# Linear attention and a token/channel mixer: token mixing two slots sooner, phi of q behind it, loads in one burst per batch

## The chip, the core and the metric

The kernel runs on one core of one Trainium2 chip. The metric is device time of one execution in microseconds (us). The kernel before takes 286.91 us, the median of three runs (286.29 to 287.79).

A core has TensorE (PE, matrix products), VectorE (DVE) and ScalarE (ACT) for elementwise work, GpSimd (POOL) and SyncE (SP). Here POOL and SP issue transfers; each engine works through its own instructions in the order in which they were written. Matrix products are written to PSUM and read from there by VectorE or ScalarE.

## What is computed

Linear attention for 8 batches, 8 heads, 576 tokens and 64 columns a head; then a mixer over tokens and channels:

```python
def phi(x): return np.where(x > 0, x, np.exp(x) - 1.0) + 1.0
q_p, k_p = phi(q), phi(k)
kv  = einsum('bhsd,bhse->bhde', k_p, v)
z   = sum(k_p, axis=2)
x   = einsum('bhsd,bhde->bhse', q_p, kv) / (einsum('bhsd,bhd->bhs', q_p, z) + 1e-6)
# x as [batch, 576, 512]
h   = relu(x.T @ w_tok1) @ w_tok2        # token mixing: 576 -> 256 -> 576
u   = x + h.T
out = u + relu(u @ w_ch1) @ w_ch2        # channel mixing: 512 -> 1536 -> 512
```

Inputs and output are float32; products are made in bfloat16 and summed in float32.

## The kernel before

**Tiling.** The 576 tokens of a batch are four groups of 128 (`r` = 0 to 3) and a tail of 64. The tails of an even and the following odd batch share the two halves of one 128-row tile. q, k and v of a batch are loaded by `load` (L99), each in two halves of four heads (`g` = 0, 1) with a main and a tail transfer each, twelve transfers a batch, all issued by SP. There are two sets of raw buffers, for even and odd batches. There is one buffer each for phi of k (`kp`), phi of q (`qp`) and v in bfloat16 (`vs`); qT, x, u and uT have two.

**The work for one batch**, by helper:

- `phi` (L136): an exp on ScalarE (L116), then on VectorE y = f + 1 (L122), min (L130) and max (L131), for half a batch at a time.
- `vcast` (L141): v to bfloat16, on ScalarE by default, on VectorE where `nc.vector.tensor_copy` is given (L144, L145). `prep_k` (L392) is phi of k and then the cast of v, for one half.
- `kv` (L153): k_p times v with a column of ones, 10 matmuls of 130 columns for each half.
- `qtr` (L181) transposes phi of q on PE with copies by ScalarE, for batches up to 3; from batch 4 on `qtr_dma` (L190) does it with one crossbar transpose issued by SP.
- `nd` (L219): numerator and denominator on PE (L200), and the quotient on VectorE (L210 to L213), in six pieces.
- `mm1` (L229) and `mm2` (L240): token mixing, with ReLU on ScalarE (L238) and u = h + x on VectorE (L252; the tail, L250).
- `utr` (batches 0 and 1, on PE) or `utr_dma` (from batch 2 on, crossbar, L331): u transposed to uT in two parts; `utr_tail` or `utr_tail_dma` for the pair of tails.
- `mm3` (L343) and `mm3_tail`: first channel product and ReLU on ScalarE (L353, L362). `mm4` and `mm4_end` (L378): second channel product, sum with u on VectorE (L382), and the store of the output (by POOL, in the last pair by SP).

**The order.** No scheduler decides: the order on each engine is the order in which the Python calls stand. Batch 0 is done first, with warming matmuls between its pieces. Then comes, for each batch n, a list `big` of slots of mostly four matmuls (`mm3`, `mm3_tail`, `mm4`), and a list `fill` of pairs (slot, function). `run` (L540) calls slot i and then every fill with that number; a stable sort keeps those of one slot in the order in which they were put in the list. Into the slots of batch n go the token mixing of batch n+1 (`steps`, L520, with slots from `at0`, `at1`, `AT3` or `AT`), and phi and cast for batch n+2, or in the first stages for the next one. In this document "stage n" is that stretch. Stages 0, 2, 4 and 6 have 24 slots, stages 1, 3, 5 and 7 have 30: the tail is done there as well.

Stage n begins with mm3 of batch n, which needs uT of n and so u of n, made in stage n-1. It needs `kp` and `vs` for kv of n+1 in its first slots, and qT of n+1 for the first `nd`.

**PSUM.** `ps_big` has four banks for mm3 and mm4; a bank comes free with the ReLU or the output sum that reads it. `ps_sm` has two buffers of two banks for everything else.

**SP's queue.** Loads, crossbar transposes and, in the last pair, stores are issued in order. Eight semaphores are used in turn, so that a transfer isn't issued before the one eight places ahead of it has landed. A wait at the head of this queue holds everything behind it. In stage 2 the order before is: the loads of batches 4 and 5, the transpose of q for batch 4, both parts of uT of batch 3, q of batch 6, the tails' transpose, k and v of batch 6.

Of the kernel before, what the change touches and what calls it, by code (L numbers as in the profile page):

```python
# [18 lines left out]
def kernel(  # L19
# [17 lines left out]
    nc = tc.nc  # L37

    B, H, S, D = q.shape
# [54 lines left out]
    def after(ins, other):  # L94
        if other is not None:
            tc.add_manual_dep(ins.ins, other.ins.name, sync_dep, reason="order of transfers")
        return ins

    def load(nm, n, g, gate=None):  # L99
        b = n % 2  # L100
        hs = slice(HG * g, HG * g + HG)
        dst = raw[nm, b]
        s = src[nm][n, hs, 0:SM, :].rearrange("h (p r) d -> p h r d", r=R)
        ins = after(nc.sync.dma_start(out=dst[:, hs, 0:R, :].rearrange("p h r d -> p h (r d)"),  # L104
                                      in_=s.rearrange("p h r d -> p h (r d)")), gate)
        nc.sync.dma_start(out=dst[half[b], hs, R, :],  # L106
                          in_=src[nm][n, hs, SM:S, :].transpose([1, 0, 2]))
        return ins
# [27 lines left out]
    def phi(nm, n, h0, nh):  # L136
        phi_exp(nm, n, h0, nh)
        phi_add(nm, n, h0, nh)
        phi_end(nm, n, h0, nh)
# [97 lines left out]
        for mt in range(NT):  # L237
            nc.scalar.activation(out=ar[b][:, mt, :], in_=ps[:, mt], func=AF.Relu)  # L238

    def mm2(n, rs):  # L240
        b = n % 2
        m = len(rs)
        ps = ps_sm.tile([128, 2, DM], FP32, name="h_ps", tag="sm")
        for i, r in enumerate(rs):
            for kt in range(NT):
                nc.tensor.matmul(out=ps[:, i], lhsT=w2t[:, kt, b, :] if r == R else w2v[:, kt, r],  # L246
                                 rhs=ar[b][:, kt, :], start=(kt == 0), stop=(kt == NT - 1))
        if rs[0] == R:
            h = half[b]
            nc.vector.tensor_tensor(out=ut[n // 2 % 2][h], in0=ps[h, 0], in1=x[b][h, R], op=ALU.add)  # L250
        else:
            nc.vector.tensor_tensor(out=u[b][:, rs[0]:rs[0] + m], in0=ps[:, 0:m],  # L252
                                    in1=x[b][:, rs[0]:rs[0] + m], op=ALU.add)
# [249 lines left out]
    for g in range(2):  # L503
        landed["k1", g] = load("k", 1, g, c_in[1] if g == 0 else None)
    for g in range(2):
        landed["v1", g] = load("v", 1, g)
    for g in range(2):
        landed["q1", g] = load("q", 1, g)
    c2_in += [after(load_wc2(i), landed["v1", 1] if i == 1 else None) for i in range(1, NB)]
    for nm in "kqv":  # L510
        for g in range(2):
            load(nm, 2, g, c2_in[2] if nm == "k" and g == 0 else None)
# [7 lines left out]
    def steps(n):  # L520

        out_ = [(f"kv{g}", lambda g=g: kv(n, g)) for g in range(2)]
        if n < 4:
            out_ += [(f"qt{g}", lambda g=g: qtr(n, g)) for g in range(2)]
        for i, rs in enumerate(([0, 1], [2, 3], [4])):
            for g in range(2):
                out_.append((f"nd{i}{g}", lambda g=g, rs=rs: nd(n, g, rs)))
        out_ += [("mm1", lambda: mm1(n)), ("mm2a", lambda: mm2(n, [0, 1])),
                 ("mm2b", lambda: mm2(n, [2, 3])), ("mm2t", lambda: mm2(n, [R]))]
        if n < 2:  # L530
            out_.append(("ut", lambda: utr(n, [0, 1])))
            if n % 2:
                out_.append(("utt", lambda: utr_tail(n // 2)))
        else:
            out_ += [("uta", lambda: utr_dma(n, [0, 1])), ("utb", lambda: utr_dma(n, [2, 3]))]
            if n % 2:
                out_.append(("utt", lambda: utr_tail_dma(n // 2)))
        return out_
# [16 lines left out]
    def m4_0(kc):  # L555
        for t in range(R):
# [1 line left out]

    big = [lambda mc=mc: mm3(0, mc, range(2, 4)) for mc in range(2)] + m3(0, 2) + \
        [lambda kc=kc: m4_0(kc) for kc in range(NCH)]  # L560
    at0 = {"kv0": 11, "kv1": 11, "qt0": 14, "qt1": 15, "nd00": 16, "nd01": 17, "nd10": 18,
           "nd11": 19, "nd20": 20, "nd21": 21, "mm1": 22, "mm2a": 23, "mm2b": 23, "mm2t": 23,
           "ut": 23, "utt": 23}
    fill = [(0, w2_tails), (2, lambda: mm2(0, [R]))]
    fill += [(5, lambda: phi("k", 1, 0, HG)), (7, lambda: phi("k", 1, HG, HG)),
             (9, lambda: vcast(1, 0, nc.vector.tensor_copy)),
             (11, lambda: vcast(1, 1, nc.vector.tensor_copy))]
    fill += [(at0[nm], fn) for nm, fn in steps(1) if nm[:2] == "kv"]
    fill += [(12, lambda: phi("q", 1, 0, HG)), (12, lambda: phi("q", 1, HG, HG))]
    fill += [(at0[nm], fn) for nm, fn in steps(1) if nm[:2] in ("qt", "nd", "mm")]  # L570
    fill += [(23, lambda: mm4_end(0, 0))]
    fill += [(at0[nm], fn) for nm, fn in steps(1) if nm[:2] == "ut"]
    fill += [(23, lambda t=t: mm4_end(0, t)) for t in range(1, R)]
# [2 lines left out]

    load_all(3, "kvq")
    big = m3(1) + m3t + m4(0, [4, 5, 6, 7, 8])
    at1 = {"kv0": 10, "kv1": 11, "qt0": 12, "qt1": 13, "nd00": 14, "nd01": 15, "nd10": 16,
           "nd11": 17, "nd20": 18, "nd21": 19, "mm1": 21, "mm2a": 23, "mm2b": 24, "mm2t": 26,  # L580
           "uta": 23, "utb": 24}
    fill = [(s, lambda g=g: prep_k(2, g, nc.vector.tensor_copy)) for g, s in ((0, 2), (1, 4))]
    fill += [(s, lambda g=g: phi("q", 2, HG * g, HG)) for g, s in ((0, 7), (1, 9))]
    fill += [(at1[nm], fn) for nm, fn in steps(2)]
    fill += [(s, lambda g=g: prep_k(3, g)) for g, s in ((0, 20), (1, 22))]
    fill += [(s, lambda g=g: phi("q", 3, HG * g, HG)) for g, s in ((0, 26), (1, 28))]
    fill += [(28, lambda: load_all(4, "qkv"))]
    run(big, sorted(fill, key=lambda e: e[0]))
    load_all(5, "qkv")

    AT3 = {"kv0": 0, "kv1": 1, "qt0": 2, "qt1": 3, "nd00": 4, "nd01": 5, "nd10": 6, "nd11": 7,
           "nd20": 8, "nd21": 9, "mm1": 11, "mm2a": 13, "mm2b": 14, "mm2t": 16, "uta": 13,
           "utb": 14, "utt": 16}
    AT = {"kv0": 0, "kv1": 1, "nd00": 3, "nd01": 4, "nd10": 5, "nd11": 6, "nd20": 7, "nd21": 8,
          "mm1": 10, "mm2a": 12, "mm2b": 13, "mm2t": 15, "uta": 12, "utb": 13, "utt": 15}
    for n in range(2, B):
        p, b = divmod(n, 2)
        if b == 0:
            big = m3(n) + m4(p, [0, 1, 2, 3])
        else:  # L600
            big = m3(n) + m3t + m4(p, [4, 5, 6, 7, 8] if n + 1 < B else [8, 4, 5, 6, 7])
        fill = []
        if n + 2 < B:
            fill += [(s, lambda g=g: phi("q", n + 2, HG * g, HG)) for g, s in ((0, 9), (1, 11))]
            fill += [(11, lambda: qtr_dma(n + 2))]
        if n + 1 < B:
            fill += [((AT3 if n == 2 else AT)[nm], fn) for nm, fn in steps(n + 1)]
        if n + 2 < B:
            fill += [(15, lambda: load_all(n + 4, "q"))]
            for g, s in ((0, 17), (1, 19)):  # L610
                fill += [(s, lambda g=g: prep_k(n + 2, g))]
            fill += [(20, lambda: load_all(n + 4, "kv"))]
        run(big, sorted(fill, key=lambda e: e[0]))

# [28 lines left out]
```

## Time and profile before

| what | value |
|---|---|
| median of 3 runs | 286.91 us (286.29 to 287.79) |
| profiled execution, in all | 288.99 us |
| its span, first to last instruction | 287.2 us |
| mean granted clock of PE over the span | 0.992 |
| exp of half a batch, ScalarE (L116) | 1273 ns |
| y, min, max of phi, VectorE (L122, L130, L131) | 821, 491, 825 ns |
| cast of half v: VectorE (L144), ScalarE (L144) | 692 ns, 1056 ns |
| u, two of four token groups, VectorE (L252) | 1219 ns |
| uT transpose, issue to landing, median of 12 | 4.5 us |

The profile is one execution. Its page lists how long each engine was busy and the chain of work that ended last, followed back from the last instruction. The timeline lists instructions in order of time: start, duration, engine and line, tiles, and in brackets how long the engine had been idle before and what released it. The view of waits lists, for one engine, who waited for what: total, times, longest. The view of one tile ends with the time from issue to landing of its transfers. The start of each stage before, read off PE's timeline at the first mm3 of a batch: stage 1 at 64.37 us, stage 2 at 101.93, stage 3 at 135.33, stage 4 at 167.92, stage 5 at 196.78, stage 6 at 229.53, stage 7 at 256.86.

The same matmul of 512 columns is shown with 379 ns, but its successor starts 216 ns later: four of them advance the chain by 0.86 us.

### The profile page before, as it was taken

Reading aid. Unit: us, or ns where it says so; the run is one execution under the profiler, and the core shown is the slowest. Engines: PE = TensorE matmul, PEld = TensorE weight load, DVE = VectorE, ACT = ScalarE, POOL = GpSimd, SP = SyncE. Lnnn points to the kernel's source line nnn. Section 1 sums busy time; section 2 is a strip of 40 time slices with the busy share of each in tenths; the row PEclk is TensorE's granted clock in tenths of the full one; section 3 lists DMA queues with packets and bytes.
Section 4 is the critical chain, followed back from the end, with each engine's and each line's share of the span. In section 5 each row is a group of like instructions: output and inputs, shape, how many; then the busy total and the mean of one; then the engine's idle time right before and its main releaser. Section 6 shows DMA issues by size and latency. Waiting matters only on the chain.

```text
span 287.2 us, 4625 instructions
## 1 busy us (share of the span) xinstructions
PE 264.2 (92%) x1784; PEld 146.8 (51%) x1804; DVE 165.3 (58%) x327; ACT 145.9 (51%) x233; POOL 29.2 (10%) x52
## 2 busy tenths in 40 slices
PE   8798978979999789897999999998999999999993
PEld 8776444544754345343556455444565454444641
DVE  4885276767877925767476718593858444520021
ACT  3664776038974337770677335943577065106400
POOL 3090020003000210002000220011000210000000
PEclk9999999999999979999999999999999999999999
DMA  6979999999701799999974994096009310340031
GB/s 209 280 109 198 281 271 177 290 282 341 220 21 52 129 276 311 289 229 267 288 211 92 252 351 150 2 192 138 2 0 189 123 37 0 69 137 34 2 110 73
DMA packets 70901, 47.98 MB, mean 167 GB/s; under 512 B 39328, under 2 KB 67872, under 8 KB 70880
## 3 DMA queue, kind: packets, MB, share of 16 engines
q1 hardware_dynamic: 64384, 36.84, 51.8%
q0 software_dynamic: 6496, 10.85, 15.7%
q8 instruction: 14, 0.23, 0.3%
q14 instruction: 7, 0.06, 0.1%
HBM read 35.85 MB, written 9.44 MB: 158 GB/s over the span
## 4 chain that ended last, share of the span: by engine, by line
PE 65%; DMA 14%; ACT 6%; SPq 5%; DVE 5%; issue 3%; POOL 1%; ACTq 0%
PE h_ps L372 25%; PE c_ps L349 23%; DMA uT<-u 6%; DMA q_raw<-in_q_dram 6%; PE a_ps L235 5%; PE h_ps L246 4%; DMA wc<-in_moe_w_ch_dram 3%; PE c_ps L360 3%; PE nd_ps L200 3%; SPq L106 3%; ACT e L116 2%; PE kv_ps L163 2%; SPq L104 2%; DVE u L252 1%; ACT cr L353 1%
## 5 line engine op out<-in xcount | busy, mean ns | idle before, releaser
L349 PE MATMUL c_ps<-uT,wc 128*128 128x512 bf16 x384 | 93.0, 382 | 7.1 <-DMA uT<-u 6.3
L353 ACT ACTIVATE cr<-c_ps 128x512 bf16<-128x512 f32 x96 | 56.3, 600 | 78.3 <-PE c_ps L349 78.3
L372 PE MATMUL h_ps<-wc,cr 128*128 128x512 bf16 x375 | 88.0, 379 | 0.8 <-DMA wc<-in_moe_w_ch_dram 0.3
L372 PEld LDWEIGHTS <-cr 128*128 128x128 bf16 x384 | 36.9, 98 | 41.6 <-issue 0.4
L349 PEld LDWEIGHTS <-wc 128*128 128x128 bf16 x384 | 35.8, 98 | 43.1 <-DMA uT<-u 5.8
L382 DVE TENSOR_TENSOR o_sb<-h_ps,u 128x512 f32<-128x512 f32 x32 | 21.5, 686 | 18.7 <-PE h_ps L372 18.7
L386 POOL DMA_DIRECT2D out_dram<-o_sb x24 | 14.4, 601 | 162.4 <-DVE o_sb L382 145.1
L213 DVE TENSOR_TENSOR x<-nd_ps,den 128x512 bf16<-128x512 f32 (+1 forms) x48 | 28.9, 603 | 1.7
L210 DVE TENSOR_SCALAR den<-nd_ps 128x8 f32<-128x8 f32 (+1 forms) x48 | 7.8, 162 | 33.7 <-PE nd_ps L200 33.2
L130 DVE TENSOR_SCALAR e<-e 128x1280 bf16<-128x1280 bf16 (+1 forms) x34 | 16.0, 471 | 14.7 <-ACT e L116 14.7
L252 DVE TENSOR_TENSOR u<-h_ps,x 128x1024 bf16<-128x1024 f32 x14 | 16.6, 1219 | 12.5 <-PE h_ps L246 12.5
L116 ACT ACTIVATE e<-k_raw 128x1280 bf16<-128x1280 f32 x16 | 20.4, 1273 | 4.2 <-DMA k_raw<-in_k_dram 4.1
L116 ACT ACTIVATE e<-q_raw 128x1280 bf16<-128x1280 f32 (+1 forms) x18 | 20.5, 1156 | 2.7 <-DMA q_raw<-in_q_dram 1.9
L200 PEld LDWEIGHTS <-qT 128*128 128x128 bf16 x160 | 12.6, 98 | 11.3 <-ACT qT L187 0.7
L200 PE MATMUL nd_ps<-kvbd,qT 128*128 128x130 bf16 x160 | 16.8, 221 | 0.7 <-ACT kvbd L167 0.5
L238 ACT ACTIVATE ar<-a_ps 128x512 bf16<-128x512 f32 x14 | 7.6, 594 | 19.2 <-PE a_ps L235 19.2
L122 DVE TENSOR_SCALAR y<-k_raw 128x1280 bf16<-128x1280 f32 x16 | 13.1, 821 | 4.7 <-DMA k_raw<-in_k_dram 4.5
L405 PE MATMUL bank<-identity 128*128 128x128 bf16 x178 | 13.6, 244 | 1.4 <-POOL identity masks.py:199 1.4
L246 PE MATMUL h_ps<-ar,w 128*128 128x512 bf16 x53 | 14.2, 379 | 0.2
L235 PE MATMUL a_ps<-x,w 128*128 128x512 bf16 x50 | 14.1, 379 | 0.3
L122 DVE TENSOR_SCALAR y<-q_raw 128x1280 bf16<-128x1280 f32 x16 | 13.2, 825 | 1.8 <-DMA q_raw<-in_q_dram 1.5
L131 DVE TENSOR_TENSOR qp<-e,y 128x1280 bf16<-128x1280 bf16 (+1 forms) x18 | 13.5, 752 | 0.6
(86 smaller groups left out, 238.2 us busy)
## 6 DMA issues: line engine op xcount, KB each, us to landing
k_raw<-in_k_dram SPq DMA_DIRECT2D x16, 512.0 KB, 7.5
q_raw<-in_q_dram SPq DMA_DIRECT2D x16, 512.0 KB, 7.4
v_raw<-in_v_dram SPq DMA_DIRECT2D x16, 512.0 KB, 8.1
out_dram<-o_sb POOLq DMA_DIRECT2D x24, 256.0 KB, 4.3
wc<-in_moe_w_ch_dram POOLq DMA_DIRECT2D x8, 384.0 KB, 8.2
out_dram<-o_sb SPq DMA_DIRECT2D x8, 256.0 KB, 2.5
k_raw<-in_k_dram SPq DMA_DIRECT2D x16, 64.0 KB, 7.1
q_raw<-in_q_dram SPq DMA_DIRECT2D x16, 64.0 KB, 6.9
```

Source lines behind the costliest of these rows:

```text
L116: nc.scalar.activation(out=e, in_=f, func=AF.Exp)
L122: nc.vector.tensor_scalar(out=y, in0=f, scalar1=1.0, scalar2=None, op0=ALU.add)
L130: nc.vector.tensor_scalar(out=e, in0=e, scalar1=1.0, scalar2=None, op0=ALU.min)
L200: nc.tensor.matmul(out=ps[:, i, a * 2 * D1:(a + 1) * 2 * D1], lhsT=qT[b][:, r, j, :], rhs=kvbd[b][:, j, :], start=True, stop=True)
L213: nc.vector.tensor_tensor(out=x[b][:, rs[0]:rs[0] + m, HG * D * g:HG * D * (g + 1)].rearrange("p r (h d) -> p r h d", h=HG), in0=v_[:, :, ...
L235: nc.tensor.matmul(out=ps[:, mt], lhsT=w1t[:, b, ms] if r == R else w1[:, r, ms], rhs=x[b][:, r, :], start=(r == 0), stop=(r == R))
L246: nc.tensor.matmul(out=ps[:, i], lhsT=w2t[:, kt, b, :] if r == R else w2v[:, kt, r], rhs=ar[b][:, kt, :], start=(kt == 0), stop=(kt == NT ...
L252: nc.vector.tensor_tensor(out=u[b][:, rs[0]:rs[0] + m], in0=ps[:, 0:m], in1=x[b][:, rs[0]:rs[0] + m], op=ALU.add)
L349: nc.tensor.matmul(out=ps, lhsT=wc1[:, kj, 128 * mc:128 * mc + 128], rhs=uT[b][:, :, kj], start=(kj == 0), stop=(kj == NDM - 1))
L353: nc.scalar.activation(out=cr[b][:, mc, :], in_=ps, func=AF.Relu)
L372: nc.tensor.matmul(out=ps, lhsT=crt[:, kc, :] if t == 8 else cr[b][:, kc, 128 * r:128 * r + 128], rhs=wc2[:, kc, :], start=(kc == 0), stop ...
L382: nc.vector.tensor_tensor(out=o, in0=ps, in1=ut[p % 2] if t == 8 else u[b][:, r, :], op=ALU.add)
```

## The change

The slots of token mixing are one to three lower in every stage. Phi of q for a batch to come, and the crossbar transpose of it, move behind the token mixing; phi of k and the cast of v move ahead of it. The twelve loads of a batch are called in one place, k v q. The loads of batch 1 are issued k q v, and the gate of the later parts of w_ch2 moves with the second pair of them. In stages 0 and 1 the cast of v comes after phi of q. For batch 1, x is added to the second half of h on PE, with an identity matrix, and ScalarE copies the sum to u.

```diff
-    def mm2(n, rs):
+    def mm2(n, rs, add=False):
...
-                                 rhs=ar[b][:, kt, :], start=(kt == 0), stop=(kt == NT - 1))
+                                 rhs=ar[b][:, kt, :], start=(kt == 0),
+                                 stop=(kt == NT - 1 and not add))
+            if add:
+                nc.tensor.matmul(out=ps[:, i], lhsT=identity, rhs=x[b][:, r, :], start=False,
+                                 stop=True)
...
+        elif add:
+            nc.scalar.copy(out=u[b][:, rs[0]:rs[0] + m], in_=ps[:, 0:m])
...
     for g in range(2):
+        landed["q1", g] = load("q", 1, g)
+    for g in range(2):
         landed["v1", g] = load("v", 1, g)
-    for g in range(2):
-        landed["q1", g] = load("q", 1, g)
-    c2_in += [after(load_wc2(i), landed["v1", 1] if i == 1 else None) for i in range(1, NB)]
+    c2_in += [after(load_wc2(i), landed["q1", 1] if i == 1 else None) for i in range(1, NB)]
...
-                 ("mm2b", lambda: mm2(n, [2, 3])), ("mm2t", lambda: mm2(n, [R]))]
+                 ("mm2b", lambda: mm2(n, [2, 3], n == 1)), ("mm2t", lambda: mm2(n, [R]))]
...
-    at0 = {"kv0": 11, "kv1": 11, "qt0": 14, "qt1": 15, "nd00": 16, "nd01": 17, "nd10": 18,
-           "nd11": 19, "nd20": 20, "nd21": 21, "mm1": 22, "mm2a": 23, "mm2b": 23, "mm2t": 23,
+    at0 = {"qt0": 12, "qt1": 13, "kv0": 14, "kv1": 14, "nd00": 15, "nd01": 16, "nd10": 17,
+           "nd11": 18, "nd20": 19, "nd21": 20, "mm1": 21, "mm2a": 23, "mm2b": 23, "mm2t": 23,
            "ut": 23, "utt": 23}
...
     fill += [(5, lambda: phi("k", 1, 0, HG)), (7, lambda: phi("k", 1, HG, HG)),
-             (9, lambda: vcast(1, 0, nc.vector.tensor_copy)),
-             (11, lambda: vcast(1, 1, nc.vector.tensor_copy))]
-    fill += [(at0[nm], fn) for nm, fn in steps(1) if nm[:2] == "kv"]
-    fill += [(12, lambda: phi("q", 1, 0, HG)), (12, lambda: phi("q", 1, HG, HG))]
-    fill += [(at0[nm], fn) for nm, fn in steps(1) if nm[:2] in ("qt", "nd", "mm")]
+             (9, lambda: phi("q", 1, 0, HG)), (11, lambda: phi("q", 1, HG, HG))]
+    fill += [(14, lambda g=g: vcast(1, g, nc.vector.tensor_copy)) for g in range(2)]
+    fill += [(at0[nm], fn) for nm, fn in steps(1) if nm[:2] in ("kv", "qt", "nd", "mm")]
...
-    at1 = {"kv0": 10, "kv1": 11, "qt0": 12, "qt1": 13, "nd00": 14, "nd01": 15, "nd10": 16,
-           "nd11": 17, "nd20": 18, "nd21": 19, "mm1": 21, "mm2a": 23, "mm2b": 24, "mm2t": 26,
-           "uta": 23, "utb": 24}
-    fill = [(s, lambda g=g: prep_k(2, g, nc.vector.tensor_copy)) for g, s in ((0, 2), (1, 4))]
-    fill += [(s, lambda g=g: phi("q", 2, HG * g, HG)) for g, s in ((0, 7), (1, 9))]
+    at1 = {"kv0": 8, "kv1": 8, "qt0": 9, "qt1": 10, "nd00": 11, "nd01": 12, "nd10": 13,
+           "nd11": 14, "nd20": 15, "nd21": 16, "mm1": 18, "mm2a": 20, "mm2b": 21, "mm2t": 23,
+           "uta": 20, "utb": 21}
+    dve = nc.vector.tensor_copy
+    fill = [(s, lambda g=g: phi("k", 2, HG * g, HG)) for g, s in ((0, 1), (1, 2))]
+    fill += [(s, lambda g=g: phi("q", 2, HG * g, HG)) for g, s in ((0, 4), (1, 6))]
+    fill += [(7, lambda g=g: vcast(2, g, dve)) for g in range(2)]
     fill += [(at1[nm], fn) for nm, fn in steps(2)]
-    fill += [(s, lambda g=g: prep_k(3, g)) for g, s in ((0, 20), (1, 22))]
-    fill += [(s, lambda g=g: phi("q", 3, HG * g, HG)) for g, s in ((0, 26), (1, 28))]
-    fill += [(28, lambda: load_all(4, "qkv"))]
+    fill += [(s, lambda g=g: prep_k(3, g)) for g, s in ((0, 17), (1, 23))]
+    fill += [(s, lambda g=g: phi("q", 3, HG * g, HG)) for g, s in ((0, 25), (1, 27))]
+    fill += [(24, lambda: load_all(4, "kvq")), (25, lambda: load_all(5, "kv")),
+             (28, lambda: load_all(5, "q"))]
     run(big, sorted(fill, key=lambda e: e[0]))
-    load_all(5, "qkv")
...
-    AT3 = {"kv0": 0, "kv1": 1, "qt0": 2, "qt1": 3, "nd00": 4, "nd01": 5, "nd10": 6, "nd11": 7,
-           "nd20": 8, "nd21": 9, "mm1": 11, "mm2a": 13, "mm2b": 14, "mm2t": 16, "uta": 13,
-           "utb": 14, "utt": 16}
-    AT = {"kv0": 0, "kv1": 1, "nd00": 3, "nd01": 4, "nd10": 5, "nd11": 6, "nd20": 7, "nd21": 8,
-          "mm1": 10, "mm2a": 12, "mm2b": 13, "mm2t": 15, "uta": 12, "utb": 13, "utt": 15}
+    AT3 = {"kv0": 0, "kv1": 0, "qt0": 1, "qt1": 2, "nd00": 3, "nd01": 4, "nd10": 5, "nd11": 6,
+           "nd20": 7, "nd21": 8, "mm1": 10, "mm2a": 12, "mm2b": 13, "mm2t": 15, "uta": 12,
+           "utb": 13, "utt": 15}
+    AT = {"kv0": 0, "kv1": 0, "nd00": 2, "nd01": 3, "nd10": 4, "nd11": 5, "nd20": 6, "nd21": 7,
+          "mm1": 9, "mm2a": 11, "mm2b": 12, "mm2t": 14, "uta": 11, "utb": 12, "utt": 14}
...
-        if n + 2 < B:
-            fill += [(s, lambda g=g: phi("q", n + 2, HG * g, HG)) for g, s in ((0, 9), (1, 11))]
-            fill += [(11, lambda: qtr_dma(n + 2))]
         if n + 1 < B:
             fill += [((AT3 if n == 2 else AT)[nm], fn) for nm, fn in steps(n + 1)]
         if n + 2 < B:
-            fill += [(15, lambda: load_all(n + 4, "q"))]
-            for g, s in ((0, 17), (1, 19)):
-                fill += [(s, lambda g=g: prep_k(n + 2, g))]
-            fill += [(20, lambda: load_all(n + 4, "kv"))]
+            d = 1 if n == 2 else 0
+            fill += [(s + d, lambda g=g: prep_k(n + 2, g)) for g, s in ((0, 8), (1, 12))]
+            fill += [(s + d, lambda g=g: phi("q", n + 2, HG * g, HG)) for g, s in ((0, 14), (1, 16))]
+            fill += [(16 + d, lambda: qtr_dma(n + 2)), (18, lambda: load_all(n + 4, "kvq"))]
```

## The prediction, made before the changed kernel was run

> **What bounds the kernel now.** First the page's busy shares, then the chain that ended last:
>
> ```profile
> PE 264.2 (92%) x1784; PEld 146.8 (51%) x1804; DVE 165.3 (58%) x327; ACT 145.9 (51%) x233; POOL 29.2 (10%) x52
> PE 65%; DMA 14%; ACT 6%; SPq 5%; DVE 5%; issue 3%; POOL 1%; ACTq 0%
> ```
>
> TensorE is the bound, so only its idle time (23 us of 287.2) and slow-clocked time can be won or lost. The waits of PE from 102 us on, then its timeline at the places where it waits:
>
> ```profile
> PE c_ps L349 <- DMA uT<-u: 6.3, 3, 3.2
> PE a_ps L235 <- DVE x L213: 1.3, 1, 1.3
> ...
> 101.93 1.89 PE L349 MATMUL c_ps<-uT,wc 128*128 128x512 bf16 x4 [3.19 <-DMA uT<-u]
> 119.66 0.38 PE L235 MATMUL a_ps<-x,w1t 128*128 128x512 bf16 x1 [1.27 <-DVE x L213]
> 135.33 1.02 PE L349 MATMUL c_ps<-uT,wc 128*128 128x512 bf16 x4 [1.70 <-DMA uT<-u]
> 196.78 1.02 PE L349 MATMUL c_ps<-uT,wc 128*128 128x512 bf16 x4 [1.37 <-DMA uT<-u]
> ```
>
> Call "stage n" the stretch in which the channel mixing of batch n runs with the token mixing of batch n+1 woven in. Three stages begin late, because uT, the transposed token-mixed activations, comes late: 3.19, 1.70 and 1.37 us. After the first, four matmuls take 1.89 us instead of 1.02: the clock is at half. The windows view gives 0.58 for 102 to 106 us; half speed over some 3.4 us costs 1.7. The fourth loss is x, late by 1.27 because a phi of q stands between its last two pieces on VectorE. Next, what feeds kv in stage 1 (VectorE, then PE), and the landings of the two transposes of q after stages 2 and 4:
>
> ```profile
> 68.95 0.49 DVE L130 TENSOR_SCALAR e<-e 128x1280 bf16<-128x1280 bf16 x1 [1.92 <-ACT e L116]
> 70.22 0.69 DVE L144 CAST vs<-v_raw 128x1024 bf16<-128x1024 f32 x1
> 73.01 0.69 DVE L144 CAST vs<-v_raw 128x1024 bf16<-128x1024 f32 x1
> 77.19 0.83 DVE L131 TENSOR_TENSOR qp<-e,y 128x1280 bf16<-128x1280 bf16 x1
> ...
> 73.86 0.39 PE L163 MATMUL kv_ps<-vs,kp 128*128 128x130 bf16 x4
> ...
> DMA to landing us min/median/max: 10.3/10.3/10.3
> ...
> DMA to landing us min/median/max: 4.9/4.9/4.9
> ```
>
> Today the cast of v stands before phi of q; VectorE runs from 68.95 to 78.02 without a pause, and kv has no wait. A transpose of q lands in 4.9 to 5.6 us, but in 10.3 when issued (121.97) straight behind 24 loads.
>
> **The Trainium skill.** "TensorE: Matmul & The Clock Gate", section "What's actually happening": the array falls to half clock after an idle window of about 3.4 us, the windows run free of the kernel, and a busy window restores it. The trace agrees: 3.19 us idle, then 3.4 us at half. Since the windows run free, an idle time near 3.4 us may or may not cost it. "DMA: Bandwidth & Descriptors", section "Issuing engines are not separate DMA queues": all transfers interleave on the same 16 engines. The 10.3 us landing beside 4.9 is that.
>
> **The change part by part.** A slot of four matmuls is 0.866 us, kv 0.57 per half, a transpose group of q 0.56, nd 0.23 (0.115 for the tail), mm1 2.16, mm2 0.216 a matmul (rows of the chain and the starts on PE's timeline). On VectorE, phi of half a batch is 2.06 (start to start 0.74 + 0.53 + 0.74 to 0.86), a cast of half v 0.8, u 1.13 to 1.2, an output sum 0.6 to 0.65. On ScalarE an exp holds 1.16 to 1.27.
>
> *Stage 0, loads k q v, phi of q before the cast.* Before: kv waits for v (1.36 and 0.29), the first transposes for qp (1.06, at 45.80), the second start at 47.92; slot 16 and the first nd are done at 49.6. After: q lands where v did (cast at 39.5 and 40.6), v where q did (43.0, 45.1). The exp of q now stands before the ReLUs of chunks 10 and 11, whose PSUM banks the next matmuls need: they start near 41.5 instead of 41.98. qp is done at 41.8 and 44.1, v cast at 45.1 and 46.1, kv ends at 46.8, where the next rows of w_ch2 land (46.85 before; their gate, the second load pair, stays in place). Slot 16 and the first nd are then done at 48.8: 0.8 won. The end: mm1 a slot sooner hides its ReLUs; the second half of u costs two more identity matmuls (0.43) and moves to ScalarE. No row has a 128x1024 copy from f32 PSUM there; the neighbours are 1.01 (uT) and 1.06 (v), I take 1.05. It runs beside the first half on VectorE instead of after it (u: 2.35 for both). From the first mm2 to stage 1 I get 5.4 against 5.66 (58.71 to 64.37). Sum -1.0 (0 to -1.5, as landings fall).
>
> *Stage 1, everything two to three slots sooner.* Both kv go from slots 10 and 11 to slot 8, phi of k starts a slot sooner, but the casts of v now stand behind both phis of q. With P the stage's start, PE is ready for kv at P + 9 x 0.866 = P+7.8. VectorE: first exp of k one ReLU sooner, P+2.4 to P+3.7; then four phis and two casts, the same run as 68.95 to 78.02: 9.07. That ends at P+12.8, the first cast at P+12.1. kv waits 4.3, its second half 0.2 more: +4.5. The small waits that filled the stage before (34.36 measured, 33.8 by adding rows) fall away: -0.4. Half clock after 4.15 us idle: from 0 to 1.7; I take 0.7. Behind kv queue every later slot and, through u, the transposes on SP. Sum +4.8 (+3.5 to +6).
>
> *End of stage 1.* mm2 comes three slots sooner: u's second half ends at P+27.8 plus the stall, its transpose lands 4.6 to 5.1 later (rows at 95.3 and 96.8), near P+32.7; PE needs it at P+33.8. The wait goes, 1 us to spare: -3.2, and -1.7 of half clock. The next loads follow right behind on SP, as they did before.
>
> *Stage 2.* phi of q no longer stands between pieces of x: -1.27. On SP, the uT transposes are no longer behind that of q (6.73 of issuing), but still behind 24 loads, which end near 121 and drain near 129 (v lands up to 8.7 after its issue). I put uT at 130 to 131, PE's need near 130.8: of the 1.70, 1.5 goes. Moving phi of k ahead costs nothing: k and v have landed about 5 us earlier, and mm1's ReLUs still precede mm2. Sum -2.8 (-1.3 to -3.0).
>
> *Stage 3, a new wait.* The transpose of q for batch 4 is now last. VectorE in stage 2 after u (at Q+20.8, Q the start): phi of k 2.06, output 0.65, tail 0.65, phi 2.06, output 0.6, phi 2.06: qp at Q+28.9. Landing 4.9 to 5.6: Q+33.9 to 34.5. The first nd of stage 3 needs it after three slots and kv: Q + 28.6 + 3.73 = Q+32.35. +1.8 (0 to +7). Behind that nd queue all of PE's work. Batch 6's loads are issued after this transpose.
>
> *Stages 4 and 5.* The wait of 1.37 goes: u ends 18.8 after the start, uT lands before 24, the stage lasts 27.5. The transpose of q starts at 26.3, lands at 31.2 to 31.9, is needed at 31.2: +0.4. Sum -1.0. Stages 3 and 5 have 30 slots, so the transposes of batches 5 and 7 land in time; stages 6 and 7 have no idle to lose. The later loads are issued 17 us or more ahead of their use.
>
> Sum: -1.0 + 4.8 - 4.9 - 2.8 + 1.8 - 1.0 = **-3.1**: the profiled span of 287.2 would be 284.1. That execution took 288.99 in all, 1.8 around its span, and is 2.1 above the median of 286.91. Whether the runs timed fall to half clock as the profiled one does is unknown; I count 1.0 rather than 1.7 for it: -2.4, **284.5 us**.
>
> **The rivals.**
> *A. The transposes stay late.* With bursts of loads right around them, uT at the ends of stages 1 and 2 lands up to 1.1 us later than I put it in each. For it: 5.1 to 5.8 us landings beside loads, 3.0 to 4.4 without. Against: the load behind them is what it was. 284.5 + 2.2 = 286.7, no change.
> *B. The transpose of q at the end of stage 2 lands as at 121.97: in 10.3 us.* The wait in stage 3 is 10.3 - 3.45 = 6.85 instead of 1.8, and at that length the clock halves: 284.5 + 5.1 + 1.7 = 291.3. Slower than before by 0.5% once the landing takes more than 7.3 us with half clock, 9 without. For it: the loads of batches 4 and 5 are on the same engines. Against: they were issued 10 us earlier, and those of batch 6 come behind.
> *C. kv doesn't wait in stage 1*, because VectorE gets through earlier: 284.5 - 5.2 = 279.3. For it: the page shows VectorE busy for only 58% of the span. Against: its 9.07 us without pause.
> That the change is not carried out can't be: the order on each engine is written out.
>
> **How the numbers follow.** Forecast 0.55 (own range 282.3 to 286.3), A 0.20, B 0.17, C 0.08. What a measurement can tell here is about 0.5%, 1.4 us. Faster: 0.49 of the forecast and C, 0.57; same: A, 0.06 of the forecast, less 0.02 of A's upper end: 0.24; slower: B and that end, 0.19. The range leaves out C and about half of B: 281.0 to 289.5.
>
> **What would show it.** PE waiting about 4.3 us for the cast of v (vcast, L144) ahead of kv in stage 1, perhaps half clock after it; no wait for uT at the starts of stages 2 and 5 and under 0.5 at stage 3; no wait for x in stage 2; PE waiting 1 to 2.5 us for the transpose of q before the first nd of stage 3, under 1 in stage 5. I am wrong if kv waits longer than 6, or if the transposes of q land in 7 us or more.

## The result, and the profile after

The changed kernel is slower: 296.14 us, median of 4 runs (294.9 to 296.91), against 287.35 for the kernel before (4 runs, 286.29 to 288.91). The ratio is 1.0297, with a 95% interval of 1.0234 to 1.0361. The prediction was 284.5 us, and its range ended at 289.5. The ratios here and below leave out the few executions that took over 1.5% longer than the fastest of the same kernel: three of the twelve of experiment 7, and one or two of the kernel before in each set of experiments.

The profiled execution after took 294.9 us with a span of 293.1, against 288.99 and 287.2 before: 5.9 us more. It was the fastest of its four, 1.2 below their median, and the profiled one of before 1.6 above its median. Together that makes the 8.8 us between the medians.

First, the page after: busy shares, the granted clock in 40 slices of 7.3 us, and the chain that ended last, by engine and by line.

```profile
PE 268.8 (92%) x1806; PEld 149.0 (51%) x1806; DVE 165.5 (56%) x326; ACT 146.7 (50%) x234; POOL 29.7 (10%) x52
...
PEclk9999999999799999998699999999799999999999
...
PE 75%; DVE 11%; DMA 7%; ACT 3%; issue 2%; SPq 0%; DVEq 0%; ACTq 0%
PE h_ps L379 28%; PE c_ps L356 24%; DMA qT<-qp 6%; PE a_ps L235 5%; PE h_ps L247 5%; PE c_ps L367 4%; PE nd_ps L200 3%; DVE y L122 3%; DVE e L130 2%; PE kv_ps L163 2%; DVE qp L131 2%; DVE kp L131 2%; DMA k_raw<-in_k_dram 1%; ACT e L116 1%; PE tp L173 1%
```

PE is still busy for 92% of a longer span, partly because matmuls at half clock count as busy for longer. The clock is low in three places, near 75, 140 and 207 us. And one transfer has come onto the chain with 6%: the transpose of q. The waits of PE from 60 us on (total, times, longest) say the same:

```profile
PE nd_ps L200 <- DMA qT<-qp: 8.2, 2, 5.3
PE kv_ps L163 <- DVE vs L144: 4.2, 1, 4.2
```

The waits for uT (6.3 us in three) and for x (1.3) are gone; a wait for the cast of v and two for the transpose of q are there instead. PE's timeline has their places, and the starts of stages 2 and 3 (start, duration, instruction; in brackets the idle time before it and what ended it):

```profile
74.32 0.40 PE L163 MATMUL kv_ps<-vs,kp 128*128 128x130 bf16 x4 [4.17 <-DVE vs L144]
...
102.15 1.03 PE L356 MATMUL c_ps<-uT,wc 128*128 128x512 bf16 x4
...
130.59 1.03 PE L356 MATMUL c_ps<-uT,wc 128*128 128x512 bf16 x4
...
139.77 0.61 PE L200 MATMUL nd_ps<-kvbd,qT 128*128 128x130 bf16 x4 [5.29 <-DMA qT<-qp]
140.17 1.91 PE L356 MATMUL c_ps<-uT,wc 128*128 128x512 bf16 x4
...
204.69 0.41 PE L200 MATMUL nd_ps<-kvbd,qT 128*128 128x130 bf16 x4 [2.89 <-DMA qT<-qp]
```

The last line but one is a stage's ordinary four matmuls taking 1.91 us instead of 1.03: half clock. The windows view of after, over stretches of 3.41 us, shows when. The three spells of half clock in this trace last 3.41, 6.83 and 3.41 us, and they begin 61.4 and 68.3 us apart, which is 18 and 20 times 3.41; the stretches are laid on this grid and are called windows below (start:end, length, busy us of PE, PEld, DVE, ACT, POOL, then the clock, the DMA share, GB/s):

```profile
68.65:72.07 3.42, 1.50 (x7) 0.49 (x5) 3.32 (x5) 3.42 (x5) 0.00 (x0) 1.00 1.09 361
72.07:75.48 3.41, 1.11 (x17) 0.94 (x18) 3.15 (x7) 1.02 (x4) 0.00 (x0) 1.00 0.99 252
75.48:78.89 3.41, 3.41 (x22) 2.21 (x20) 0.00 (x0) 1.36 (x5) 0.00 (x0) 0.50 0.06 19
...
133.51:136.92 3.41, 0.97 (x5) 0.24 (x3) 0.00 (x0) 1.19 (x2) 0.00 (x0) 1.00 1.06 232
136.92:140.33 3.41, 0.56 (x5) 0.56 (x6) 0.00 (x0) 0.00 (x0) 0.00 (x0) 0.50 1.03 240
140.33:143.75 3.42, 3.42 (x13) 1.49 (x11) 2.12 (x6) 0.60 (x1) 0.00 (x0) 0.50 1.11 306
...
201.78:205.19 3.41, 0.52 (x7) 0.39 (x7) 0.06 (x1) 0.60 (x1) 0.00 (x0) 1.00 0.57 218
205.19:208.60 3.41, 3.41 (x13) 1.49 (x12) 2.06 (x6) 0.60 (x1) 0.00 (x0) 0.50 0.00 0
208.60:212.02 3.42, 3.42 (x26) 1.92 (x25) 2.76 (x9) 1.88 (x4) 0.00 (x0) 1.00 0.00 0
```

Read each row with the next: a window in which PE is mostly idle is followed by one at half clock, and after a fully busy one the clock is full again. In stage 3 the stall is so long that two windows are at half. So a wait can cost more than its own length: 1.7 us more in stages 1 and 5 (half of a busy window of 3.41), and 2.0 in stage 3 (half of the 3.98 us from the end of the wait to 143.75).

The starts of the stages in PE's two timelines give the balance. Each stage is counted up to the first matmul of the next, so a wait for uT belongs to the stage that it ends; the predicted column is the prediction's own terms, sorted in the same way. (By this timeline stages 6 and 7 of the kernel before start at 229.37 and 256.69; the 229.53 and 256.86 given further up are 0.16 and 0.17 too late.)

| | before | after | difference | predicted |
|---|---|---|---|---|
| start of stage 1 | 64.37 | 62.22 | -2.2 | -1.0 |
| stage 1 | 37.56 | 39.93 | +2.4 | +1.6 |
| stage 2 | 33.40 | 28.44 | -5.0 | -4.5 |
| stage 3 | 32.59 | 40.00 | **+7.4** | +1.8 |
| stage 4 | 28.86 | 27.32 | -1.5 | -1.4 |
| stage 5 | 32.59 | 37.35 | **+4.8** | +0.4 |
| from stage 6 on | 57.83 | 57.84 | 0.0 | 0 |
| sum | | | +5.9 | -3.1 |

Five of the seven rows came out within 1.2 us. The whole error is in stages 3 and 5, where PE waits for the transpose of q. Why is it late? VectorE, SP and POOL around its two issues, each from its own timeline of after; first VectorE, the last step of phi of q and what comes behind it:

```profile
130.30 0.82 DVE L131 TENSOR_TENSOR qp<-e,y 128x1280 bf16<-128x1280 bf16 x1
131.04 1.28 DVE L389 TENSOR_TENSOR o_sb<-h_ps,u 128x512 f32<-128x512 f32 x2
...
196.15 0.82 DVE L131 TENSOR_TENSOR qp<-e,y 128x1280 bf16<-128x1280 bf16 x1
197.00 1.89 DVE L389 TENSOR_TENSOR o_sb<-h_ps,u 128x512 f32<-128x512 f32 x3
```

Then SP, which issues the transposes and loads:

```profile
131.19 3.08 SPq L191 DMA_TRANSPOSE qT<-qp  x1
134.36 1.24 SPq L104 DMA_DIRECT2D k_raw<-in_k_dram  x1
...
197.00 3.40 SPq L191 DMA_TRANSPOSE qT<-qp  x1
```

Then POOL, which issues the stores of the output, 256 KB each:

```profile
132.02 1.14 POOL L393 DMA_DIRECT2D out_dram<-o_sb  x2 [2.05 <-DVE o_sb L389]
...
198.00 1.73 POOL L393 DMA_DIRECT2D out_dram<-o_sb  x3 [5.12 <-DVE o_sb L389]
```

And the landings of these two transposes, from the view of tile qT in the two stretches:

```profile
DMA to landing us min/median/max: 8.5/8.5/8.5
...
DMA to landing us min/median/max: 7.6/7.6/7.6
```

The transpose is issued where the prediction put it, but lands in 8.5 and 7.6 us instead of 4.9 to 5.6. New beside it are the stores. On VectorE the output sums of the stage's last slots now queue behind phi of q; they come out in a bunch, and POOL begins to issue their stores (two, then three) within 1 us after the transpose. In the kernel before, SP and POOL have, for the transposes that landed in 5.6 and 4.9 us,

```profile
153.65 2.95 SPq L191 DMA_TRANSPOSE qT<-qp  x1
...
186.24 3.11 SPq L191 DMA_TRANSPOSE qT<-qp  x1
...
158.75 0.56 POOL L386 DMA_DIRECT2D out_dram<-o_sb  x1 [23.41 <-DVE o_sb L382]
...
189.34 0.57 POOL L386 DMA_DIRECT2D out_dram<-o_sb  x1 [19.18 <-DVE o_sb L382]
```

There the first stores come 5.1 and 3.1 us behind the transposes. Whether the stores, the loads behind the transpose, or something else delay it was the question for the experiments.

### The profile page after: what moved, and what is told of

The parts are those of the page before. It is cut to its first block, busy times and chain, and to the rows that moved or that the text cites. A ratio compares the mean times of both kernels' runs of the same rounds, so it can differ in the third digit from the quotient of the medians.

```text
span 293.1 us, 4648 instructions
## 1 busy us (share of the span) xinstructions
PE 268.8 (92%) x1806; PEld 149.0 (51%) x1806; DVE 165.5 (56%) x326; ACT 146.7 (50%) x234; POOL 29.7 (10%) x52
## 4 chain that ended last, share of the span: by engine, by line
PE 75%; DVE 11%; DMA 7%; ACT 3%; issue 2%; SPq 0%; DVEq 0%; ACTq 0%
PE h_ps L379 28%; PE c_ps L356 24%; DMA qT<-qp 6%; PE a_ps L235 5%; PE h_ps L247 5%; PE c_ps L367 4%; PE nd_ps L200 3%; DVE y L122 3%; DVE e L130 2%; PE kv_ps L163 2%; DVE qp L131 2%; DVE kp L131 2%; DMA k_raw<-in_k_dram 1%; ACT e L116 1%; PE tp L173 1%
## 5 line engine op out<-in xcount | busy, mean ns | idle before, releaser
L356 PE MATMUL c_ps<-uT,wc 128*128 128x512 bf16 x384 | 95.6, 391 | 0.8 <-ACT uT L328 0.7
L356 PEld LDWEIGHTS <-wc 128*128 128x128 bf16 x384 | 36.8, 100 | 37.8 <-issue 3.8
L213 DVE TENSOR_TENSOR x<-nd_ps,den 128x512 bf16<-128x512 f32 (+1 forms) x48 | 28.9, 602 | 1.7
L259 DVE TENSOR_TENSOR u<-h_ps,x 128x1024 bf16<-128x1024 f32 x13 | 15.9, 1225 | 23.6 <-PE h_ps L247 23.6
L200 PE MATMUL nd_ps<-kvbd,qT 128*128 128x130 bf16 x160 | 17.5, 228 | 8.7 <-DMA qT<-qp 8.2
L200 PEld LDWEIGHTS <-qT 128*128 128x128 bf16 x160 | 13.2, 102 | 20.0 <-DMA qT<-qp 9.2
L412 PEld LDWEIGHTS <-identity 128*128 128x128 bf16 x178 | 13.0, 114 | 1.4 <-POOL identity masks.py:199 1.4
```

Of the source, the lines that this page charges most:

```text
L200: nc.tensor.matmul(out=ps[:, i, a * 2 * D1:(a + 1) * 2 * D1], lhsT=qT[b][:, r, j, :], rhs=kvbd[b][:, j, :], start=True, stop=True)
L213: nc.vector.tensor_tensor(out=x[b][:, rs[0]:rs[0] + m, HG * D * g:HG * D * (g + 1)].rearrange("p r (h d) -> p r h d", h=HG), in0=v_[:, :, ...
L356: nc.tensor.matmul(out=ps, lhsT=wc1[:, kj, 128 * mc:128 * mc + 128], rhs=uT[b][:, :, kj], start=(kj == 0), stop=(kj == NDM - 1))
L412: nc.tensor.matmul(out=ps[:, 0:128], lhsT=identity, rhs=identity, start=True, stop=True)
```

## The experiments

Each is compared with the kernel before in runs on the same chip. Differences to the changed kernel are against its 296.14 from the first set of runs; the kernel before had medians of 287.2 to 288.2 in the four sets, so such a difference is good to about 1 us. What is read from a trace is read from one profile of each kernel.

**1. The cast of v ahead of phi of q in stage 1 again.** The rest of the change stays.

```diff
-    fill = [(s, lambda g=g: phi("k", 2, HG * g, HG)) for g, s in ((0, 1), (1, 2))]
+    fill = [(s, lambda g=g: prep_k(2, g, dve)) for g, s in ((0, 1), (1, 2))]
...
-    fill += [(7, lambda g=g: vcast(2, g, dve)) for g in range(2)]
```

> The changed kernel, but in stage 1 the casts of v stand right behind the phi of k that they belong to, ahead of phi of q. Theory (the 4.2 us wait of kv in stage 1, and the half clock after it, come from the place of the casts alone): that wait falls under 0.7, some 0.4 to 0.6 us of waits for phi of q appear before the two transpose groups instead, no half clock in stage 1; 4 to 5.5 us shorter than the changed kernel, so 290.6 to 292.2. Rival (stage 1 is too early for VectorE whatever the order): the wait moves to the transposes of q in nearly full length, over 3 us, and the time falls by less than 2 us.

Measured: 291.66 us (4 runs), 1.0146 of before (1.0088 to 1.0205), 4.5 less than the changed kernel. PE's timeline in stages 1 and 3:

```profile
74.28 0.72 PE L173 MATMUL tp<-identity,qp 128*128 128x128 bf16 x10 [0.89 <-ACT kvbd L167]
...
76.10 0.73 PE L173 MATMUL tp<-identity,qp 128*128 128x128 bf16 x10 [0.24 <-DVE qp L131]
...
136.15 0.61 PE L200 MATMUL nd_ps<-kvbd,qT 128*128 128x130 bf16 x4 [5.19 <-DMA qT<-qp]
```

The wait of kv is gone, and with it the half clock of stage 1; two short waits, 0.89 and 0.24, take its place. Stage 1 lasts 35.37 us instead of 39.93. So the order of cast and phi costs 4.5 us; the waits for qT stay.

**2. The stores after the transpose.** The five stores of the last slots of stages 2 and 4 wait until the transpose of q has landed (`after` makes one DMA wait for another). Computation and order are otherwise those of the changed kernel.

```diff
...
-            put.dma_start(
+            st = put.dma_start(
                 out=out[2 * p + b, 0:SM, :].rearrange("(p r) d -> r p d", r=R)[r], in_=o)
+            if (p, t) in ((1, 2), (1, 3), (2, 1), (2, 2), (2, 3)):
+                after(st, live["qtr"])
```

> The changed kernel, but the output stores that follow the transpose of q in stages 2 and 4 (two and three of them) wait until it has landed. Theory (these stores, issued within 1 us of the transpose, make it land late): the transposes of stages 2 and 4 land in 5 to 6 us instead of 8.5 and 7.6, PE's waits at the starts of stages 3 and 5 fall from 5.3 to about 2.5 and from 2.9 to about 0.8, and the half clock goes in stage 5 at least; 5 to 8 us shorter than the changed kernel. Rival 1 (the loads of batch 6 do it): stage 2's stays at 8 us or more, and only stage 4's, which has no loads, moves. Rival 2 (a transpose this late is slow by itself): both stay.

Measured: 286.59 us (18 runs), 0.9964 of before (0.9942 to 0.9986), 9.5 less than the changed kernel and more than the 5 to 8 expected. The landings of the transposes of stages 2 and 4, and PE's timeline in stages 3 and 5:

```profile
DMA to landing us min/median/max: 4.9/4.9/4.9
...
DMA to landing us min/median/max: 5.2/5.2/5.2
...
136.30 0.41 PE L201 MATMUL nd_ps<-kvbd,qT 128*128 128x130 bf16 x4 [1.66 <-DMA qT<-qp]
...
196.85 0.41 PE L201 MATMUL nd_ps<-kvbd,qT 128*128 128x130 bf16 x4 [0.44 <-DMA qT<-qp]
```

Compare 5.29 and 2.89. These are the waits that the prediction had (1.8 and 0.4), without half clock behind them. The loads were left where they were, so with stores held the loads alone don't make the transpose late. The stores of stages 3 and 5 were not held, and they too come 0.9 us behind a transpose of q: it landed in 8.3 and 9.0 us there, but it has slots to spare, and nothing waited.

The other profiles say the same. The eleven traces of this case hold 44 such transposes. Where no store is issued from 1 us before the transpose to 3 us behind it, and no load is in flight when it is issued, it lands in 4.8 to 5.6 us (16 of them), also with loads issued 3.1 us or more behind it. With one store 0.9 us behind it (stage 4 of experiments 4 and 5), it takes 6.4; with two, 7.0 (experiment 3); with three within 2.2 us, 7.5 to 7.7; with three within 2.6 us and more to follow (stages 3 and 5), 8.1 to 10.5. Loads in front count as well: the four that were issued with loads still in flight (stage 2 of the kernel before and of experiments 4, 5 and 7) took 6.1 to 10.3.

**3. The loads after the transpose.** The first load of batch 6, and so all those behind it on SP, waits for the transpose of stage 2; the stores are as in the changed kernel.

```diff
...
-                    load(nm, n, g)
+                    load(nm, n, g, live["qtr"] if n == 6 and nm == nms[0] and g == 0 else None)
```

> The changed kernel, but the loads of batch 6 wait until the transpose of q of stage 2 has landed. Theory (the stores): that transpose still lands in 7 us or more, PE's wait at the start of stage 3 is at least 4 us, and the time is within 1.5 us of the changed kernel. Rival (the loads): it lands in 5 to 6 us, the wait falls to about 2.5 us. Stage 5 is the same as in the changed kernel under both.

Measured: 293.35 us (2 runs), 1.022 of before (1.0122 to 1.0318). PE's timeline in stage 3:

```profile
138.37 0.41 PE L201 MATMUL nd_ps<-kvbd,qT 128*128 128x130 bf16 x4 [3.77 <-DMA qT<-qp]
```

The transpose lands in 7.0 us instead of 8.5 (8.4 and 8.5 in experiments 1 and 6, which leave it as it was). The expectation of a theory that named the stores alone was missed by a little: the wait fell below 4, and 2.8 us were gained where at most 1.5 were expected. In the profile, stage 3 is 1.8 us shorter, and stage 5, which the edit doesn't touch, 1.9: its wait of 2.71 happened to fall so that PE was busy for 1.48 us of the 3.41 of that window, and no half clock followed. So the loads add about 1.5 us to the landing, but only beside the stores; without them (experiment 2) it lands in 4.9 with the loads in place. Two runs are few for the size.

**4. Phi of q and its transpose ahead of phi of k in stages 2 to 5.** Again only the order, and the load of q first.

```diff
-    fill += [(24, lambda: load_all(4, "kvq")), (25, lambda: load_all(5, "kv")),
+    fill += [(24, lambda: load_all(4, "qkv")), (25, lambda: load_all(5, "kv")),
...
-            fill += [(s + d, lambda g=g: prep_k(n + 2, g)) for g, s in ((0, 8), (1, 12))]
-            fill += [(s + d, lambda g=g: phi("q", n + 2, HG * g, HG)) for g, s in ((0, 14), (1, 16))]
-            fill += [(16 + d, lambda: qtr_dma(n + 2)), (18, lambda: load_all(n + 4, "kvq"))]
+            fill += [(s + d, lambda g=g: phi("q", n + 2, HG * g, HG)) for g, s in ((0, 8), (1, 12))]
+            fill += [(12 + d, lambda: qtr_dma(n + 2))]
+            fill += [(s + d, lambda g=g: prep_k(n + 2, g)) for g, s in ((0, 14), (1, 16))]
+            fill += [(18, lambda: load_all(n + 4, "qkv"))]
```

> The changed kernel, but from stage 2 on phi of q and its transpose take the slots of phi of k and the casts, and these take the slots of phi of q; q is loaded first. Token mixing keeps its earlier slots. Theory (the loss of stages 3 and 5 is the transpose of q being last, not the earlier token mixing): no wait of PE for qT, none for uT over 0.5 us, stages 3 and 5 last 32.5 to 33 us instead of 40.0 and 37.4; 11 to 12.5 us shorter than the changed kernel, 283.5 to 285.5. Rival (VectorE is short of time in stages 2 and 4 in any order): kv waits 1 to 4 us for phi of k or the cast at the starts of stages 3 and 5, and the time falls by less than 9 us.

Measured: 283.27 us (4 runs), 0.9879 of before (0.9832 to 0.9925), 12.9 less than the changed kernel and a little more than the 11 to 12.5 expected. The longest waits of PE from 60 us on:

```profile
PE kv_ps L163 <- DVE vs L144: 4.2, 1, 4.2
PE tp L334 <- ACT uT L274: 0.7, 1, 0.7
```

No wait for qT, and for uT only the 0.7 that the changed kernel has as well. Stages 3 and 5 take 32.59 and 32.60 us, as in the kernel before. So all that stages 3 and 5 lost goes with the place of the transpose of q (and of its load, which this edit moves along); what is left is the loss in stage 1, a wait of 4.2 and the half clock after it.

**5. Both: experiments 1 and 4 together.**

> Both reorderings together: in stage 1 the casts of v before phi of q, and from stage 2 on phi of q with its transpose before phi of k. Theory (the two losses are separate, and the earlier token mixing keeps its gain): no wait of PE for qT or of kv for the cast, no half clock after the start; about 283.3 - 4.5 = 278.8 us, between 278 and 280, some 3% faster than before. Rival (with one loss gone the next wait shows, uT at the start of stage 2 or qT before nd): 281 us or more.

Measured: 278.86 us (6 runs, 278.68 to 279.97), 0.9717 of before (0.9689 to 0.9746). The waits of PE from 60 us on, all of them:

```profile
PE tp L173 <- ACT kvbd L167: 0.9, 1, 0.9
PE tp L334 <- ACT uT L274: 0.7, 1, 0.7
PE tp L270 <- ACT u L257: 0.5, 1, 0.5
PE tp L173 <- DVE qp L131: 0.2, 1, 0.2
```

And the page:

```profile
PE 262.8 (95%) x1806; PEld 146.4 (53%) x1806; DVE 164.9 (60%) x326; ACT 147.1 (53%) x234; POOL 29.3 (11%) x52
...
PEclk9999999999999999999999999999999999999999
```

This beats both kernels: the same 1806 matmuls as the changed kernel take 6.0 us less of PE, 5.4 of them the half clock that is gone. It keeps what the change won (stage 2 at 28.44, stage 4 at 27.33, no wait for the landing of uT) and drops its two mistakes of order.

**6. Keeping the clock up.** The transposes stay late; ahead of the first nd of stages 3 and 5 PE runs 80 and 45 matmuls of the identity, whose result is overwritten.

```diff
...
+        if (n, g, rs[0]) in ((4, 0, 0), (6, 0, 0)):
+            for _ in range(80 if n == 4 else 45):
+                nc.tensor.matmul(out=ps[:, 0, 0:128], lhsT=identity, rhs=identity, start=True,
+                                 stop=True)
```

> The changed kernel with 80 and 45 small matmuls of the identity matrix put before the first nd of stages 3 and 5, where PE waits for the transpose of q; their result isn't used. Theory (what is lost there is the wait, 5.3 and 2.9 us, plus half clock afterwards, 2.0 and 1.7 us): the first nd comes no later than in the changed kernel, the clock stays full after both, and the time falls by 3 to 4.5 us, to 291.5 to 293. Rival (half clock in the records is no loss of time): the time stays within 1 us of the changed kernel's.

Measured: 293.11 us (4 runs), 1.0198 of before (1.0157 to 1.024), 3.0 less than the changed kernel, at the edge of what was expected. The first nd is no later than without them, 9.14 us after the start of stage 3 (9.18 in the changed kernel) and 6.74 in stage 5 (6.78), and the clock is full behind both. Stage 3 is 2.0 us shorter and stage 5 1.7: the half clock as read from the windows. In this profile's stage 1, which the edit doesn't touch, half clock held for two windows instead of one, and the stage took 40.45 us instead of 39.93.

**7. The part in stage 0 alone,** added to the kernel before: the loads of batch 1 as k q v, phi of q ahead of the cast, x added on PE, the lower slots of stage 0.

```diff
...
-    at0 = {"kv0": 11, "kv1": 11, "qt0": 14, "qt1": 15, "nd00": 16, "nd01": 17, "nd10": 18,
-           "nd11": 19, "nd20": 20, "nd21": 21, "mm1": 22, "mm2a": 23, "mm2b": 23, "mm2t": 23,
+    at0 = {"qt0": 12, "qt1": 13, "kv0": 14, "kv1": 14, "nd00": 15, "nd01": 16, "nd10": 17,
+           "nd11": 18, "nd20": 19, "nd21": 20, "mm1": 21, "mm2a": 23, "mm2b": 23, "mm2t": 23,
...
-                 ("mm2b", lambda: mm2(n, [2, 3])), ("mm2t", lambda: mm2(n, [R]))]
+                 ("mm2b", lambda: mm2(n, [2, 3], n == 1)), ("mm2t", lambda: mm2(n, [R]))]
```

> The kernel before with only the stage 0 part of the change: the loads of batch 1 in the order k q v, its slots of stage 0, and x added on PE for the second half of u. Theory (this part wins what the starts of stage 1 show, 62.2 against 64.4 us, and keeps it to the end): 1.5 to 2.5 us faster than before. Rival (the gain is given back at the start of stage 2, where PE waits for uT whose chain through VectorE and ScalarE doesn't start earlier): under 0.7 us.

Measured: 287.37 us (12 runs), 0.9962 of before (0.9933 to 0.9991): about 1 us won, less than the theory's 1.5 to 2.5 and more than the rival's 0.7. Stage 1 starts at 63.00, but in PE's timeline stage 2 then starts with

```profile
101.53 1.89 PE L356 MATMUL c_ps<-uT,wc 128*128 128x512 bf16 x4 [4.16 <-DMA uT<-u]
```

The wait for uT is 4.16 instead of 3.19, with half clock over two windows behind it: most of what stage 0 won is given back at the end of stage 1, which this kernel has as before. The size of the gain at stage 0 itself stays unsettled: in the profiles of the kernels with this stage 0, stage 1 starts anywhere from 62.22 (the changed kernel) to 64.38 (experiment 6). The mean of these ten is 63.2, 1.2 us ahead of the one profile of the kernel before, and close to the 1.0 predicted.

**8. The same stores from SP's queue.** No store waits for a landing. The five stores are issued by SP, behind the transpose, instead of by POOL.

```diff
-        put = nc.sync if p == B // 2 - 1 else nc.gpsimd
+        put = nc.sync if p == B // 2 - 1 or (p, t) in (
+            (1, 2), (1, 3), (2, 1), (2, 2), (2, 3)) else nc.gpsimd
```

> The changed kernel, but the five output stores that follow the transposes of q in stages 2 and 4 are issued by SP, where they stand behind the transpose (in stage 2 behind the loads of batch 6 too), instead of by POOL at once. Nothing waits for a landing. Theory (the stores do harm because they come through a second queue and take turns with the transpose on the same engines; behind it in one queue they come after it): stage 4's transpose lands in 5 to 6 us, PE's wait at the start of stage 5 is under 1 us, stage 3's about 2. Rival (any store in flight slows it): stage 4's still lands in 7 us or more and PE waits over 2 us in stage 5.

Measured: 286.52 us (10 runs), 0.9961 of before (0.993 to 0.9992), as in experiment 2. Both transposes land in 4.9 us. SP's timeline at the end of stage 4:

```profile
193.09 3.48 SPq L191 DMA_TRANSPOSE qT<-qp  x1
196.67 1.50 SPq L394 DMA_DIRECT2D out_dram<-o_sb  x3
```

The issue of a transpose holds SP for 3.5 us here, so the stores leave 3.6 us after the transpose began to be issued instead of 1. The Trainium skill, "DMA: Bandwidth & Descriptors", section "Queues, rings and completion order", says that each DMA engine takes turns, packet by packet, between the queues that have work for it. That fits: stores of another queue get turns against the transpose, stores of its own come behind it. But here they are later as well as in the same queue, and this run doesn't tell the two apart. The kernel before adds a hint for the time alone: there the store of 189.34 came through POOL's queue, 3.1 us behind the transpose of 186.24, and that still landed in 4.9.

**9. Experiments 1 and 2 together.**

> The changed kernel with the casts of v ahead of phi of q in stage 1 and the five stores held until the transpose of q has landed; the order of phi of q and phi of k stays as changed. Theory (the two losses add up): 286.6 - 4.5 = about 282.1 us, 281 to 283.5, with about 1.7 and 0.4 us of waits for the transposes left. Rival (they don't, because kv's wait gave the transfers time to clear): 284.5 or more.

Measured: 280.58 us (4 runs), 0.9754 of before (0.9706 to 0.9802), a little better than expected. The single gains were 4.5 and 9.5, together 15.6 came, 1.6 more than their sum of 14.0: neither loss hides the other. Where the 1.6 come from is not shown. The 1.7 between this and experiment 5 are about the 1.65 and 0.39 us that PE still waits for qT here.

## Why the prediction was wrong

*What bounds the kernel*: right. What stages 1 to 5 won and lost was PE's idle and half-clocked time; from stage 6 on nothing changed.

*Stage 0*: -1.0 predicted, -2.2 in the pair of profiles, about -1 over the whole kernel when done alone. The sign is right, the size not settled; the mean over ten profiles (1.2, experiment 7) speaks for about 1. The copy of u on ScalarE, taken as 1.05, took 1.01.

*Stage 1*: the wait of kv was 4.17 for 4.3, behind the cast of v, as worked out. The half clock was counted as 0.7, between 0 and 1.7; it was 1.7. Experiment 1 shows wait and clock together as 4.5.

*End of stage 1 and stage 2*: right. The wait for uT (3.19) and the half clock after it are gone, the wait for x and the 1.70 at stage 3 too; stage 2 took 5.0 less for 4.5. *Stage 4*: right, -1.5 for -1.4.

*Rival A*, transposes of u still late: fell; no wait for their landing is left. *Rival C*, kv doesn't wait: fell.

*"Stage 3, a new wait"* is the step that failed, and with it the +0.4 of stage 5. The mechanism was named and the moment was right: the transpose was expected at Q+28.9 and issued at 131.19, with Q at 102.15, which is Q+29.0. In stage 4 it was expected 26.3 after the start and came after 26.4. The term that was mis-sized is the landing: taken from the transposes of before as 4.9 to 5.6, it was 8.5 and 7.6, past the 7 us that the prediction itself had named as the sign of being wrong. Those transposes had their first stores 3 to 5 us behind their issue, not 1. (Stages 3 and 5 came out right in spite of landings of 9.1 and 8.7: the slots to spare hid the same error there.) The prediction followed the loads on SP past the transpose but not what its own reordering did to POOL: its sum "phi, output, tail, phi, output, phi" on VectorE already held the outputs, and the ones that follow the last phi come out in a bunch right at the transpose. Experiment 2 shows that with the stores held back the waits are 1.66 and 0.44, so the rest of that step was right to 0.2 us. The second half of the error is that a step given as "+1.8 (0 to +7)" had no half clock in its middle or at its end, though the same text priced it for stage 1: it added 2.0 and 1.7 (experiment 6). Stage 3 so cost 7.4 instead of 1.8 and stage 5 4.8 instead of 0.4: 10 us. With these 10 added, the predicted -3.1 becomes +6.9, against +5.9 in the pair of profiles.

*Rival B* had the right shape, transpose late and then half clock, at 291.3 us. Its cause was wrong: it blamed the loads of batches 4 and 5, and by the trace of the changed kernel all of these had landed when the transpose was issued at 131.19. For that reason it saw the loss in stage 3 only, while stores also meet the transpose of stage 4, for which stage 5 waits. Nor was the 10.3 a fixed price of loads in front: in experiment 7, with the same loads in the same order and six still in flight as in the kernel before, that transpose landed in 6.4. That B came so near in time in stage 3 was therefore luck. What could have been seen beforehand is that the place left 3.45 us for a landing of 4.9 or more, so that every microsecond of delay there would be paid in full.

What stays open: whether it is the separate queue or the start within 1 us that lets the stores delay the transpose, since the issue of a transpose of q held SP for 2.95 us or more each time and so nothing on SP's own queue could start that early; and the size of stage 0's gain.

## What to carry to other kernels

When a step is moved behind another on an engine, list what is then released just after it, on every queue, stores included: the landing of a transfer that is needed at once must not be taken from transfers that had no such neighbours. A wait of PE of nearly 3 us or more is priced with the half clock that may follow it (1.7 to 2.0 us here), wherever it stands in the sum. Of two preparations that share VectorE, the one with a long transfer behind it (phi of q) goes first, and the one that feeds PE directly (the cast of v in stage 1) goes ahead of what is needed later: these two changes of order were worth 17 us here, about twice what the rest of the change won (experiment 5 is 2.8% faster than the kernel before).

## What the runs showed of the hardware

Two or three stores of 256 KB from POOL's queue, issued within 1 us of a crossbar transpose of 128x2560, made it land in 7.0 to 8.5 us instead of 4.9; one such store, in experiments 4 and 5, made it 6.4. Loads issued behind it on its own queue added about 1.5 of this, and only beside the stores. The issue of such a transpose held SP for 2.95 to 6.7 us.

The windows that bring half clock don't need to be idle throughout. In the changed kernel's trace, a window with PE idle for 56% of it (1.50 busy of 3.42) was followed by full clock, one idle for 67% (1.11 of 3.41) by half. A wait of 2.89 us, shorter than a window but wholly inside one (201.80 to 204.69), left it 85% idle and cost 1.7 more. In experiment 3 a wait of 2.71 at the same place left its window 57% idle and cost no more than itself. So the same wait can be dear or not, as it falls on the windows.
